# Output of the third column block between the last weight pieces, and another order for the first three attention steps

## The chip, the cores and the metric

The kernel runs on one core of one Trainium2 chip. The metric is the device time of one execution in microseconds (us), as the median of several runs. A profile is one further execution, recorded by the hardware profiler.

## The reference

Windowed attention over a sequence of 768, with the sequence also seen as 24 block summaries of 32 positions each, and behind it a soft mixture of experts. All arithmetic is float32.

```python
k_sum = k.reshape(B, H, nb, 32, D).max(axis=3)           # B,H,S,D = 4,8,768,64; nb = 24
v_sum = v.reshape(B, H, nb, 32, D).mean(axis=3)
scores_l = where(|i-j| < 16, scale * q @ k.T, -1e9)
scores_s = scale * q @ k_sum.T + log(32)
a = softmax(concat([scores_l, scores_s]))                # a / (sum + 1e-9)
x = (a @ concat([v, v_sum])) as [3072, 512]
logits = x @ phi                                         # phi 512 x 32 slots, 8 experts x 4
slot_in = softmax(logits, axis=0).T @ x
slot_out[e] = relu(slot_in[e] @ w1[e]) @ w2[e]           # w1 512 x 1024, w2 1024 x 512
out = softmax(logits, axis=1) @ slot_out                 # 3072 x 512
```

## The kernel before, in words

**The order is written out by hand.** Each engine runs its instructions in the order in which the program issues them (`tc.manual_schedule()`, line 834); semaphores are set from the tiles that are written and read. So a wait of one instruction holds everything behind it on the same engine. All large transfers are issued by SyncE (SP) and share its queue, also in program order; only the constants `cs` come from ScalarE's (line 510).

**Attention: 24 steps.** A step `i` is one third of the queries of four heads (`hb = i // 3`, `tp = i % 3`). Its parts, by the helper that issues them:

- `scores(i)` (line 226): 32 matmuls into two PSUM tiles s0 and s1. Each exists once, so `scores(i+1)` waits until VectorE has read those of step i. A query tile meets its own 64 keys, 32 neighbours and 24 block maxima. The neighbours and the maxima lie in an extra area of `kk` that `k_edge` (line 193) and `k_put` (line 205) fill, for two values of `c` and six query tiles; `scores(i)` reads the query tiles `2*tp` and `2*tp+1`. `k_max` (line 181) finds the maxima on VectorE, in six parts per `hb`.
- `soft_max(i, r)` (line 244) on VectorE for r = 0 and 1, four instructions each, which read s and leave the masked scores and their maximum in SBUF. For r = 0 `soft_exp` (line 259) follows with four ScalarE instructions; for r = 1 GpSimd first subtracts the maximum (`soft_sub`, line 267) and one ScalarE instruction does the rest.
- In the step after: `put_v` (line 347) on GpSimd writes the block sums of v into the tile of values, `trans` (line 271) transposes on TensorE, `evac` (line 278) copies back on ScalarE.
- Two steps after: `values` (line 283) and `norm` (line 301).
- `V0` to `V7`: `v_sum(hb)` (line 320), the block sums of v for one `hb`: 48 matmuls that need the three tiles of values of that `hb`, a copy on ScalarE (line 337), two additions on VectorE into `vsst` (line 340). `PLAN` (line 41) says at which step such pieces begin; the part of an entry in front of the bar is begun and finished in the middle of the step, the part behind the bar is begun at the step's end and finished in the next step, ahead of `soft_max` of r = 1. X, L, T and D are pieces of the routing to experts, later on.

Before the steps stand seven warm-up products (line 506), the first loads (lines 507 to 516), and for `hb` 0 the maxima (line 524), edges (GpSimd, line 525) and `k_put` (VectorE, line 526), then a clearing of `W1ST` on GpSimd (line 527).

**The end.** The first expert layer is 32 weight pieces (line 667), the second is done in three column chunks, a (256 columns, 16 pieces), b and c (128 columns, 8 pieces each). The generator `stage2` (line 695) gives one piece per advance, then three closing advances: a scaling on VectorE (`sos`, line 715), a product on TensorE (`so2`, line 718), a copy on VectorE into `sls` (line 720). `combine` (line 724) makes the output from `sls`, for each block of 128 columns in four advances: the four matmuls of part 0 (256 wide) with two ScalarE copies; two VectorE copies and the output transfer (512 KB); the four matmuls of part 1 (512 wide) with two ScalarE copies; two VectorE copies and two output transfers of 512 KB (four of 256 KB for the very last part). A is two blocks, B and C one each. Six PSUM buffers serve these products. The string `END` (line 68) is the order in which all are advanced: a lower-case letter advances `stage2`, an upper-case one `combine`, the digits of `c1 c2 c3` only mark the closing advances.

Of the kernel before, what the change touches and what calls it, by code (L numbers as in the profile page):

```python
# [16 lines left out]
B, H, S, D = 4, 8, 768, 64  # L17
NT, DM, NS, NE, DF = B * S, H * D, 32, 8, 1024
NB = S // 32
# [3 lines left out]
NTT = 2 * TPS  # L23
# [15 lines left out]


PLAN = {
    0: "| V0",
    2: "| V1",
    5: "| V2",
    6: "X0 X1 |",
# [20 lines left out]

CHUNKS = {"a": (0, 256), "b": (256, 128), "c": (384, 128)}
END = (
    "a a a a a a a a a a a a a a a a a1 b b a2 b b a3 b b A A b A A b A A c A A c b1 c b2 c b3 c "
    "c c c c1 B c2 c3 B B B C C C C"  # L70
)


# [1 line left out]
def attention_soft_moe(  # L75
# [12 lines left out]
    nc = tc.nc  # L88
# [66 lines left out]
    def load_k(hb, pr=None):  # L155
        if hb < HB:
            k = kk[hb % 2][:, K0:EA0]
            c = slice(0, 2 * KP) if pr is None else slice(KP * pr, KP * pr + KP)
            nc.sync.dma_start(out=k[:, c], in_=kx[hb, :, c])

    def load_q(i):
        if i < NSTEP:
            nc.sync.dma_start(out=qb[:, i % NQR], in_=qx[i // TPS, :, i % TPS])

    def load_v(i):
        if i < NSTEP:
            v = vs[i % NV]
            nc.sync.dma_start(out=v.rearrange("p c t h d -> p (c t h d)"), in_=vx[i, :, 0:1040])


    def kview(hb):
        k = kk[hb % 2][:, K0:EA0]
        return k.rearrange("p (r k) -> p r k", r=2)

    def eview(hb, c):
        e0 = (EA0, 0)[c]
        return kk[hb % 2][:, e0 : e0 + NEH].rearrange("p (r t k) -> p r t k", r=2, t=NTT)

    kst = {}

    def k_max(hb, part):
        if hb >= HB:
            return
        if hb not in kst:
            kst[hb] = wk.tile([128, 2, NB], F32, name="ks", bufs=2)
        pr, th = part // 3, part % 3
        nc.vector.reduce_max(  # L187
            out=kst[hb][:, pr, 8 * th : 8 * th + 8],
            in_=kview(hb)[:, pr, 16 + 256 * th : 272 + 256 * th].rearrange("p (b k) -> p b k", k=32),
            axis=AX,  # L190
        )

    def k_edge(hb, eng):
        if hb >= HB:
            return
        k = kview(hb)
        for c in range(2):
            e = eview(hb, c)[:, :, :, 32 * c : 32 * c + 32]
            for half in range(2):
                o = 64 * c + 80 * half  # L200
                src = k[:, :, o : o + 128 * (NTT - 1) + 16]
                src = bass.AP(src.tensor, src.offset, [src.ap[0], src.ap[1], [128, NTT], [1, 16]])
                eng.tensor_copy(out=e[:, :, :, 16 * half : 16 * half + 16], in_=src)  # L203

    def k_put(hb, eng):
        if hb >= HB:
            return
        for c in range(2):
            o = 0 if c else 32
            eng.tensor_copy(  # L210
                out=eview(hb, c)[:, :, :, o : o + NB], in_=kst[hb].unsqueeze(2).broadcast_to([128, 2, NTT, NB])
            )

    def keys(hb, r, c, pr, t):
# [11 lines left out]
    def scores(i):  # L226
        hb, tp = steps[i]
        s = [ps_s.tile([128, 4, 128], F32, name=f"s{r}") for r in range(2)]
        for u in range(4):
            tt, pr = u // 2, u % 2  # L230
            for r in range(2):
                for c in range(2):
                    o = 128 * tt + 64 * c
                    nc.tensor.matmul(  # L234
                        s[r][64 * c : 64 * c + 64, u, :].rearrange("p (a k) -> p a k", a=2),
                        lhsT=qb[64 * r : 64 * r + 64, i % NQR, pr, o : o + 64],
                        rhs=keys(hb, r, c, pr, 2 * tp + tt),
                        start=True,
                        stop=True,
                        tile_position=(64 * r, 64 * c),  # L240
                    )
        ps_[i] = s
# [104 lines left out]
    def put_v(i, c, eng):  # L347
        n0 = 0 if c else 96
        src = vsst[0:NB, i // TPS % 2].rearrange("n h c -> n (h c)").unsqueeze(1)
        eng.tensor_copy(  # L350
            out=vs[i % NV][n0 : n0 + NB, c].rearrange("n t h c -> n t (h c)"), in_=src.broadcast_to([NB, 2, 260])
        )
# [129 lines left out]
    def advance(g):  # L482
        try:
            next(g)
            return True
        except StopIteration:
            return False

    def flush(gs):
        for g in gs:  # L490
            while advance(g):
                pass
# [3 lines left out]
    def begin(names):  # L496
        gs = [pieces_of[n[0]](int(n[1:])) for n in names.split()]
        for g in gs:
            advance(g)
        return gs  # L500
# [7 lines left out]
    load_k(0, 1)  # L508
    load_q(0)
    nc.scalar.dma_start(out=cs, in_=cst)  # L510
    for i in range(TPS):
        load_v(i)
    load_q(1)
    load_q(2)
    load_k(1, 0)
    load_k(1, 1)
# [6 lines left out]
    for part in range(6):  # L523
        k_max(0, part)
    k_edge(0, nc.gpsimd)
    k_put(0, nc.vector)
    nc.gpsimd.memset(W1ST, 0.0)


# [1 line left out]
    for i in range(NSTEP):  # L531
        a, b = i - 1, i - 2
        front, back = (PLAN.get(i, "|")).split("|")
        hb, tp = i // TPS, i % TPS
        now[0] = i
        scores(i)
        if i < TPS:
            for n in ((3, 4), (5,), (6,))[i]:
                load_v(n)
        if i == 0:  # L540
            load_q(3)
        load_q(i + NQR)
        if tp == 2:
            load_k(hb + 2, 0)
        if tp == 0 and hb > 0:
            load_k(hb + 1, 1)
        held = [g for g in held if advance(g)]
        soft_max(i, 0)
        soft_exp(i, 0)
        flush(held)  # L550
        if a >= 0:
            for c in range(2):
                put_v(a, c, nc.gpsimd)
        for n in range(LOADS[i]):
            if now[0] < 19:
                load_piece(True)
        if tp == 2:
            k_put(hb + 1, nc.gpsimd)
        soft_max(i, 1)
        if i < NSTEP - 1:  # L560
            soft_sub(i, 1)
        if tp == 1:
            k_edge(hb + 1, nc.gpsimd)
        if a >= 0:
            trans(a, 0)
            trans(a, 1)
            evac(a, 0)
            evac(a, 1, nc.vector.tensor_copy if i == NSTEP - 1 else None)
        flush(begin(front))
        soft_exp(i, 1)  # L570
        if b >= 0:
            values(b)
            norm(b)
        if tp < 2:
            for part in ((0, 1, 2), (3, 4, 5))[tp]:
                k_max(hb + 1, part)
        held = begin(back)
        if b >= 0:
            load_v(b + NV)
        for _ in range(LOADS[i]):  # L580
            if now[0] >= 19:
                load_piece()
# [80 lines left out]
    for k in range(32):  # L663
        _, e, c = pieces[k]
# [17 lines left out]
    for i in range(2):  # L682
        nc.vector.tensor_copy(
            out=W2ST[i].rearrange("p j (e k) -> p j e k", e=NE)[:, :, :, 0:4],
            in_=ph[:, 128 * i : 128 * i + 128].rearrange("p (j e k) -> p j e k", j=4, e=NE),
# [157 lines left out]
```

## Time and profile before

| | us |
|---|---|
| median of three runs | 193.09 |
| the three runs | 193.09, 191.21, 193.20 |
| the profiled execution's own time | 191.26 |
| its span, first to last instruction | 189.0 |
| mean granted TensorE clock in the span | 0.976 of full |

The span begins with the first instruction and ends with the last; the 2.3 us between it and the execution's own time lie around it. All times below count from the span's start. A step's end is read as the end of its last VectorE instruction that reads scores.

### The profile page before, as it was taken

The numbers are of one execution on the slowest core, as the hardware profiler recorded it, in microseconds if no ns is written. First come the engines' busy times: TensorE is split into PE (matmuls) and PEld (weight loads), VectorE is DVE, ScalarE is ACT, GpSimd is POOL, SyncE is SP. The second block draws the span as 40 slices with busy tenths as digits, with TensorE's granted clock in tenths as the row PEclk, the third lists the DMA queues.
The fourth block names the chain that finished last, engine by engine and source line by source line (L and its number), as shares of the span: only waits on it lengthen the run. The fifth ranks groups of instructions, "written<-read, shape, count | busy, mean of one in ns | idle before, by whom it ended". The sixth has DMA issues, their size and how long they took to land.

```text
span 189.0 us, 7987 instructions
## 1 busy us (share of the span) xinstructions
PE 165.9 (88%) x3201; PEld 130.0 (69%) x3201; DVE 121.1 (64%) x626; ACT 94.4 (50%) x244; POOL 71.9 (38%) x147
## 2 busy tenths in 40 slices
PE   6596999998999979899999898989779989998940
PEld 5394877976968967697798696878357755664720
DVE  1758599686879688848978885864567610135450
ACT  2026667587676677756678577765301000033240
POOL 3425956748544943824854844420020000000000
PEclk9969999999999999999999999999999999999985
DMA  5999989998799998979899999979999999999697
GB/s 193 415 401 400 344 336 299 385 393 312 223 368 386 304 355 262 352 231 297 290 264 389 402 408 408 388 275 394 416 409 404 402 413 408 406 401 396 251 397 269
DMA packets 20628, 66.35 MB, mean 351 GB/s; under 512 B 2288, under 2 KB 2288, under 8 KB 20592
## 3 DMA queue, kind: packets, MB, share of 16 engines
q1 hardware_dynamic: 20448, 65.48, 93.0%
q8 instruction: 25, 0.41, 0.9%
q10 hardware_dynamic: 144, 0.37, 0.5%
q14 instruction: 11, 0.09, 0.1%
HBM read 59.55 MB, written 6.29 MB: 348 GB/s over the span
## 4 chain that ended last, share of the span: by engine, by line
PE 55%; DVE 12%; ACT 12%; issue 4%; POOL 3%; DMA 2%; DVEq 1%; POOLq 0%; ACTq 0%; SPq 0%
PE s L234 8%; PE o L291 8%; PE pt L275 8%; PE hps L667 7%; PE so L705 6%; PE pp L327 5%; DVE p L253 5%; ACT xt L364 4%; PE pp L361 3%; ACT ptr L280 3%; PE op L731 3%; DMA out<-wa 2%; ACT p L263 2%; PE pp L374 2%; PE pp L417 2%
## 5 line engine op out<-in xcount | busy, mean ns | idle before, releaser
L263 ACT ACTIVATE p<-p,m 128x128 f32<-128x128 f32 x100 | 32.0, 391 | 27.3 <-DVE m L253 27.3
L253 DVE CUSTOM_DVE_ANT_0 p<-s,cs 128x128 f32<-128x128 f32 x192 | 42.6, 286 | 4.4 <-PE s L234 4.1
L269 POOL TENSOR_TENSOR p<-m,p 128x512 f32<-128x512 f32 x23 | 23.9, 1038 | 44.0 <-DVE m L253 28.1
L234 PE MATMUL s<-kk,q 64*64 64x128 f32 x768 | 29.9, 280 | 4.2 <-DVE kk L210 2.2
L350 POOL COPY v<-vsst 24x520 f32<-24x520 f32 x48 | 29.4, 612 | 4.4 <-issue 1.6
L234 PEld LDWEIGHTS s<-kk,q 64*64 64x64 f32 x768 | 24.0, 136 | 10.2 <-issue 4.7
L291 PE MATMUL o<-v,ptr 120*64 120x65 f32 (+1 forms) x768 | 27.9, 225 | 1.5 <-DVE x L312 0.9
L291 PEld LDWEIGHTS o<-v,ptr 120*64 120x64 f32 (+1 forms) x768 | 24.6, 138 | 5.6 <-issue 4.6
L275 PE MATMUL pt<-ident,p 128*128 128x128 f32 x192 | 27.9, 282 | 0.6 <-ACT p L265 0.2
L280 ACT COPY ptr<-pt 128x512 f32<-128x512 f32 x47 | 24.7, 571 | 1.7 <-PE pt L275 1.7
L275 PEld LDWEIGHTS pt<-ident,p 128*128 128x128 f32 x192 | 20.4, 140 | 6.2 <-issue 3.3
L187 DVE TENSOR_REDUCE ks<-kk 128x8 f32<-128x256 f32 x48 | 17.0, 410 | 4.3 <-DMA kk<-kx 4.2
L265 ACT ACTIVATE p<-p 128x512 f32<-128x512 f32 x23 | 14.7, 639 | 8.8 <-POOL p L269 8.7
L312 DVE TENSOR_TENSOR x<-o,z 128x256 f32<-128x256 f32 x48 | 18.1, 419 | 0.8
L253 DVE DVE_READ_ACCUMULATOR2_ANT m<- 128x1 f32 x192 | 15.9, 83 | 0.0
L327 PE MATMUL pp<-v,cs 64*64 64x128 f32 x384 | 14.0, 284 | 0.8 <-ACT xt L364 0.7
L327 PEld LDWEIGHTS pp<-v,cs 64*64 64x64 f32 x384 | 12.0, 141 | 1.6 <-ACT xt L364 1.2
L361 PE MATMUL pp<-ident,x 128*128 128x128 f32 x88 | 11.6, 273 | 0.1
L309 DVE TENSOR_SCALAR z<-o 128x8 f32<-128x8 f32 x24 | 4.0, 165 | 11.8 <-PE o L291 11.2
L364 ACT COPY xt<-pp 128x512 f32<-128x512 f32 x21 | 11.4, 595 | 0.0
L203 POOL COPY kk<-kk 128x192 f32<-128x192 f32 x32 | 9.6, 342 | 4.3 <-DMA kk<-kx 4.3
L742 ACT COPY wa<-op 128x256 f32<-128x256 f32 (+1 forms) x3 | 1.2, 445 | 20.0 <-PE op L731 20.0
(134 smaller groups left out, 199.9 us busy)
## 6 DMA issues: line engine op xcount, KB each, us to landing
wa<-w SPq DMA_DIRECT2D x40, 512.0 KB, 7.7
v<-vx SPq DMA_DIRECT2D x24, 520.0 KB, 6.1
kk<-kx SPq DMA_DIRECT2D x16, 400.0 KB, 5.3
q<-qx SPq DMA_DIRECT2D x24, 256.0 KB, 4.8
v<-w SPq DMA_DIRECT2D x7, 512.0 KB, 6.2
kk<-w SPq DMA_DIRECT2D x6, 512.0 KB, 6.9
x<-w SPq DMA_DIRECT2D x5, 512.0 KB, 7.5
out<-v SPq DMA_DIRECT2D x3, 512.0 KB, 4.8
```

The source lines that it names most:

```text
L234: nc.tensor.matmul(s[r][64 * c : 64 * c + 64, u, :].rearrange("p (a k) -> p a k", a=2), lhsT=qb[64 * r : 64 * r + 64, i % NQR, pr, o : o + ...
L253: nc.vector.tensor_tensor_reduce(out=p[:, u, :], in0=s[:, u, :], in1=maskv[:, mk, :], scale=-0.125, scalar=-NEG, op0=ALU.add, op1=ALU.min, ...
L263: nc.scalar.activation(out=p[:, u, :], in_=p[:, u, :], func=AF.Exp, scale=-1.0, bias=m[:, u : u + 1])
L269: nc.gpsimd.tensor_tensor(out=p, in0=m.unsqueeze(2).broadcast_to([128, 4, 128]), in1=p, op=ALU.subtract)
L275: nc.tensor.transpose(pt[:, u, :], p[:, u, :], ident)
L280: (eng or nc.scalar.copy)(out=ptr, in_=ptr_[i, r])
L291: nc.tensor.matmul(o[64 * c : 64 * c + 64, r, u, :], lhsT=ptr[0:K, u, 64 * c : 64 * c + 64], rhs=v[0:K, c, tt, 2 * pr + r, :], start=True, ...
L312: nc.vector.tensor_tensor(out=x[:, r], in0=o[:, r, :, 0:64].rearrange("p (t q) d -> p t q d", t=2), in1=z[:, r].rearrange("p (t q) -> p t ...
L327: nc.tensor.matmul(pv[c][64 * g : 64 * g + 64, 0:128].rearrange("p (h d) -> p h d", h=2), lhsT=cs[64 * c : 64 * c + 64, o : o + 64], rhs=v ...
L350: eng.tensor_copy(out=vs[i % NV][n0 : n0 + NB, c].rearrange("n t h c -> n t (h c)"), in_=src.broadcast_to([NB, 2, 260]))
L361: nc.tensor.transpose(pv[:, 128 * c : 128 * c + 128], x, ident)
L364: (nc.vector.tensor_copy if on_dve else nc.scalar.copy)(out=xt.rearrange("p c t -> p (c t)"), in_=pv)
```

## The change

`END`: of the four advances of B that stood behind `c1`, three are moved up between the last pieces of chunk c, and the fourth stays between `c1` and `c2`. C follows right behind `c3`.

The start: the queries of step 1 are loaded ahead of the three value tiles. `k_put(0)` is split: query tiles 0 and 1 stay on VectorE, tiles 2 to 5 go to GpSimd, ahead of the clearing of `W1ST`. `V0` moves from the end of step 0 into step 1, behind `soft_sub(1, 1)`, and `put_v(0)` follows it there. For `hb` 1 the maxima move from the ends of steps 0 and 1 to the end of step 1 and into step 2, and `k_put(1)` and `k_edge(1)` both stand in step 2 behind `soft_sub(2, 1)`. From step 3 on the order is as before.

```diff
 PLAN = {
-    0: "| V0",
+    1: "V0 |",
...
-    "... b A A c A A c b1 c b2 c b3 c "
-    "c c c c1 B c2 c3 B B B C C C C"
+    "... b A A c A A c b1 c b2 c b3 c B c B c "
+    "B c c1 B c2 c3 C C C C"
...
-    def k_put(hb, eng):
+    def k_put(hb, eng, t0=0, n=NTT):
...
             eng.tensor_copy(
-                out=eview(hb, c)[:, :, :, o : o + NB], in_=kst[hb].unsqueeze(2).broadcast_to([128, 2, NTT, NB])
+                out=eview(hb, c)[:, :, t0 : t0 + n, o : o + NB],
+                in_=kst[hb].unsqueeze(2).broadcast_to([128, 2, n, NB]),
             )
...
+    load_q(1)
     for i in range(TPS):
         load_v(i)
-    load_q(1)
...
-    k_put(0, nc.vector)
+    k_put(0, nc.vector, 0, 2)
+    k_put(0, nc.gpsimd, 2, 4)
     nc.gpsimd.memset(W1ST, 0.0)
...
-        if a >= 0:
+        if a > 0:
             for c in range(2):
                 put_v(a, c, nc.gpsimd)
...
-        if tp == 2:
+        if tp == 2 and hb > 0:
             k_put(hb + 1, nc.gpsimd)
         soft_max(i, 1)
         if i < NSTEP - 1:
             soft_sub(i, 1)
-        if tp == 1:
+        if i == 1:
+            flush(begin(front))
+            front = ""
+            put_v(0, 0, nc.gpsimd)
+            put_v(0, 1, nc.gpsimd)
+        if i == 2:
+            for part in (3, 4, 5):
+                k_max(1, part)
+            k_put(1, nc.gpsimd)
+        if tp == 1 and hb > 0:
             k_edge(hb + 1, nc.gpsimd)
+        if i == 2:
+            k_edge(1, nc.gpsimd)
...
+        if i == 1:
+            for part in (0, 1, 2):
+                k_max(1, part)
-        if tp < 2:
+        if tp < 2 and hb > 0:
             for part in ((0, 1, 2), (3, 4, 5))[tp]:
                 k_max(hb + 1, part)
```

## Rows read from the trace of the kernel before

**Rows 1.** The page's first part: busy us of each engine, with its share.

```profile
PE 165.9 (88%) x3201; PEld 130.0 (69%) x3201; DVE 121.1 (64%) x626; ACT 94.4 (50%) x244; POOL 71.9 (38%) x147
```

**Rows 2.** Stretches of the start (columns: us, busy, granted clock, DMA share, GB/s).

```profile
6.84:9.04 2.20, 0.00 (x0) 0.03 (x1) 2.17 (x5) 0.00 (x0) 1.94 (x5) 1.00 1.02 420
...
9.14:12.54 3.40, 3.40 (x63) 3.35 (x67) 1.28 (x12) 0.93 (x4) 0.00 (x0) 0.50 1.04 399
...
15.00:18.00 3.00, 1.36 (x21) 0.94 (x25) 2.86 (x20) 1.96 (x6) 1.59 (x3) 1.00 1.04 404
```

**Rows 3.** Timeline 7 to 11 us (start us, us, engine, line, operation, count).

```profile
7.43 0.34 POOL L203 COPY kk<-kk 128x192 f32<-128x192 f32 x1
...
7.56 1.38 DVE L210 COPY kk<-ks 128x288 f32<-128x288 f32 x1
...
7.72 1.06 POOL L527 MEMSET W1ST<- 128x1152 f32 x1
...
8.86 0.29 DVE L210 COPY kk<-ks 128x288 f32<-128x288 f32 x1
...
9.04 2.02 PE L234 MATMUL s<-kk,q 64*64 64x128 f32 x29 [2.21 <-DVE kk L210]
```

**Rows 4.** Timeline, DVE and ScalarE of steps 0, 1 and 3.

```profile
12.97 0.08 DVE L253 DVE_READ_ACCUMULATOR2_ANT m<- 128x1 f32 x1
...
14.75 0.24 ACT L337 COPY vp<-pp 88x128 f32<-88x128 f32 x1
...
15.09 0.58 DVE L340 TENSOR_TENSOR vsst<-pp,vp 24x128 f32<-24x128 f32 x2 [0.65 <-ACT vp L337]
...
24.36 0.29 DVE L253 CUSTOM_DVE_ANT_0 p<-s,cs 128x128 f32<-128x128 f32 x1
...
26.05 0.09 DVE L253 DVE_READ_ACCUMULATOR2_ANT m<- 128x1 f32 x1
```

**Rows 5.** Timeline 18 to 28 us: one undisturbed instance of each operation.

```profile
18.61 1.20 POOL L203 COPY kk<-kk 128x192 f32<-128x192 f32 x4
...
21.05 1.54 PE L327 MATMUL pp<-v,cs 64*64 64x128 f32 x48
...
21.11 0.79 POOL L210 COPY kk<-ks 128x288 f32<-128x288 f32 x2
...
21.87 1.03 POOL L269 TENSOR_TENSOR p<-m,p 128x512 f32<-128x512 f32 x1
...
22.41 1.05 PE L234 MATMUL s<-kk,q 64*64 64x128 f32 x32
...
23.40 1.09 PE L275 MATMUL pt<-ident,p 128*128 128x128 f32 x8
...
24.69 1.28 ACT L263 ACTIVATE p<-p,m 128x128 f32<-128x128 f32 x4 [0.98 <-DVE m L253]
...
27.16 1.06 DVE L187 TENSOR_REDUCE ks<-kk 128x8 f32<-128x256 f32 x3
```

**Rows 6.** Timeline of the end, 171 to 183 us.

```profile
171.02 1.14 PE L731 MATMUL op<-lt,sls 32*128 32x512 f32 x8
...
176.63 0.71 PE L731 MATMUL op<-lt,sls 32*128 32x256 f32 x8
...
176.77 0.35 DVE L715 TENSOR_SCALAR sos<-so,rz 128x128 f32<-128x128 f32 x1 [2.06 <-PE so L705]
...
177.80 0.29 DVE L720 COPY sls<-so 128x128 f32<-128x128 f32 x1 [0.68 <-PE so L718]
...
181.44 1.29 DVE L747 COPY v<-op 128x512 f32<-128x512 f32 x2 [0.55 <-PE op L731]
```

**Rows 7.** Stretches of the end (columns as in the second group).

```profile
177.50:179.80 2.30, 2.30 (x16) 1.75 (x17) 1.81 (x5) 1.46 (x4) 0.00 (x0) 1.00 0.25 96
...
179.80:187.60 7.80, 1.94 (x12) 1.06 (x10) 2.38 (x5) 1.84 (x5) 0.00 (x0) 0.72 1.01 394
```

**Rows 8.** The line that issues the output (min/median/max ns, first and last start).

```profile
L751 SPq DMA_DIRECT2D out<-kk x3: 332/333/685, 173.0 to 178.8; - x3
```

More of the change, by code (lines that the diff above doesn't have):

```diff
@@ L68 @@
 END = (
-    "a a a a a a a a a a a a a a a a a1 b b a2 b b a3 b b A A b A A b A A c A A c b1 c b2 c b3 c "
-    "c c c c1 B c2 c3 B B B C C C C"
+    "a a a a a a a a a a a a a a a a a1 b b a2 b b a3 b b A A b A A b A A c A A c b1 c b2 c b3 c B c B c "
+    "B c c1 B c2 c3 C C C C"
 )
```

## The prediction

> **What bounds the kernel now.** I read the page's first part, then the start and the end as timelines, then both as stretches. TensorE is busy for 165.9 of 189.0 us [rows 1]; from step 3 on it hardly pauses, so what makes step 3 earlier should make everything behind it earlier. Two places are left where TensorE or the transfers stand still.
>
> The start. TensorE does nothing from 6.84 to 9.04 us, and the granted clock, 1.00 until then, is 0.50 from 9.14 to 12.54, the lower of its two levels (1.2 GHz) [rows 2]. What ends the pause is the second copy of `k_put(0)` on VectorE. Its first copy takes 1.38 us and the second, of the same shape, 0.29 [rows 3]: the first begins while GpSimd is in its last `k_edge` copy and ends 0.16 us after GpSimd's clearing of `W1ST` (7.72 + 1.06 = 8.78), so it stood behind GpSimd for about 1.09 us. Later VectorE ends step 0 at 13.05 and can begin step 1 only at 15.7, behind V0's additions (15.09 + 0.58), which waited for a ScalarE copy of V0 [rows 4].
>
> The end. From 177.5 to 179.8 the transfers run at a share of 0.25, 96 GB/s; from 179.8 to 187.6 at 394 GB/s, with nothing left for TensorE after the first quarter [rows 7]. The last stretch, 7.8 us, is the output of B and C (2 × 1.57 MB, 8.0 us at that rate): B's first transfer is issued only at 178.8 [rows 8], and the stream picks up about 1.0 us after it.
>
> **Part 1: the first scores.** VectorE's share of `k_put(0)` falls to a third, two copies of 96 elements. Undisturbed, a copy of 288 takes 0.29, so the two cost at most 0.3 together at one third to one half of that each. Whether they are undisturbed is the question, since GpSimd now goes from its last `k_edge` copy to two copies of its own, 192 elements, 0.34 each and 0.29 apart as `k_edge` shows, and then to the clearing. If VectorE gets in behind the `k_edge` copy, at 7.77, it is done at 8.1, or at 8.4 if one GpSimd copy comes between its two; scores begin 0.6 to 0.9 us earlier than 9.04. If it again stands behind all that GpSimd has queued, that ends at 7.72 + 2 × 0.29 + 1.06 = 9.36, VectorE ends near 9.6, and scores are 0.5 us late. So the bounds are −0.9 and +0.5. I take −0.7: before, GpSimd's next instruction waited for nothing and only wrote; now it waits for the maxima as VectorE does, and reads.
>
> The Trainium skill (SBUF — State Buffer, section "Who interferes with whom") says that GpSimd and a VectorE copy of this kind share one pair of ports under an exclusive lock, and that issue order decides who blocks. The first copy agrees with the lock: 1.38 us against 0.29. It does not quite agree with the order, as VectorE asked at 7.56 and the clearing began at 7.72, yet the clearing went first; By the order of asking VectorE's two copies would end at 8.1 and the term be −0.9; by the order of the row, at 9.6 and +0.5, which is the second rival below.
>
> Query tiles 2 to 5, now GpSimd's, are ready by 8.4 to 8.7 and not read before step 1. `load_q(1)` is moved past three value loads on SP: the values land later by 262 KB, 0.6 us at about 410 GB/s, and V0, their first reader, now comes about one step later. Both cost nothing.
>
> **Part 2: steps 0 to 3.** I count from E0, the end of step 0's maxima on VectorE (13.05 before), with the durations of [rows 5].
>
> Before: step 3 ends at 26.14 [rows 4], E0 + 13.1.
>
> Changed. Step 1's scores start at E0 and take 1.1; VectorE has nothing else queued and runs step 1's eight instructions from E0+1.1 to 2.9 (1.78, as step 3 took from 24.36 to 26.14 [rows 4]). TensorE does V0 under it (1.54, to E0+2.7) and the transposes (1.09, to 3.8). ScalarE must finish step 1's four exponentials (1.28, to 3.1), then V0's copy (0.24); VectorE adds from 3.45 to 4.05, then three parts of maxima (1.06) to 5.1. Scores of step 2 are ready at 4.9; VectorE runs step 2 from 5.1 to 6.9. GpSimd does `put_v(0)` and `put_v(1)` between 4.1 and 6.7, then `soft_sub(2, 1)` (1.03) from 7.0 to 8.05, `k_put(1)` (0.79) to 8.85, whose maxima VectorE has ready at 8.0, and `k_edge(1)` (1.20) to 10.05. Scores of step 3, which need these edges, run from 10.2 to 11.25, and step 3's maxima from 11.25 to 13.0. So step 3 ends at E0 + 13.0, as before: the gap behind step 0 is closed (step 1 starts 1.1 behind E0, not 2.6), but the edges for `hb` 1, which GpSimd made early, are now at the end of its queue, and TensorE, through with V1 at E0+8.65, waits 1.5 us for them. The reorder by itself brings 0 (bounds −0.6, if GpSimd's queue runs with no gaps, and +0.7, if one `put_v` or the values of V1, loaded in a saturated stretch, come late). What it does is carry E0 on; and the scores of step 0 set E0.
>
> **The clock.** Before, step 0's scores ran at the lower level: 2.02 us for 29 matmuls [rows 3] against 1.05 for 32. With the pause cut to 1.4 us they may run at full speed, −0.9. But V0 no longer follows them: TensorE pauses again for the 1.8 us of step 0's maxima. The stretch from 15 to 18, busy for 1.36 of 3.0 us, kept its 1.00 [rows 2], the one from 6.84 did not. The new stretch of two pauses lies between; I take it that one of the two score blocks runs at the lower level, as one did before: 0, with −0.9 and +0.9 as bounds.
>
> **Part 3: the end.** Before, chunk c's last matmul ended by 176.77, where VectorE scales it [rows 6]. B's matmuls, 0.71 and 1.14, now come ahead of it, so the scaling is at 176.77 + 1.85 = 178.6 and ends at 178.95. Then VectorE has B's fourth advance queued, two copies of 512, 1.29 as the last pair took, and only then the copy into `sls`, 0.29: 180.55. The product `so2` hides under the copies; TensorE has nothing left to fill this with and stands still for some 1.5 us. C's first matmuls end at 181.3, its first output leaves near 182.0, and its last copies (1.29, behind a pair half as wide) end near 183.4.
>
> What it buys is in the transfers. B's first 512 KB is issued near 176.8 and goes into the gap, right behind A. B's other two are issued at 179.7 and 180.3, about where they were, as VectorE's copies wait behind the scaling. The stream therefore picks up at about 180.6 and has 2.62 MB left, 6.65 us at 394 GB/s: 187.2, against 187.6. I take −0.4. Bounds: −1.3, if B's first transfer is saved in full; +0.9, if C's own copies, one microsecond later, set the end.
>
> **Sum.** −0.7 (first scores) + 0 (reorder) + 0 (clock) − 0.4 (end) = −1.1. Against the profiled execution's own 191.26 (span 189.0 and 2.3 around it) that is 190.2. The executions shown stand at two levels, 191.2 and 193.1 to 193.2, two of four at each, with the median of the three runs, 193.09, on the upper. I start from their mean, 192.2: **191.1 us**.
>
> **The rivals.**
>
> *Full speed in both score blocks.* The forecast with −0.9 for the clock: −2.0, 190.2 us. For it: the longest pause of TensorE becomes 1.8 instead of 2.2. Against it: two pauses follow closely. Chance 0.18.
>
> *VectorE stays behind GpSimd's queue.* It decides once VectorE's copies end after 9.15, where they ended before; nothing in [rows 3] excludes it, since there VectorE lost the one boundary between two GpSimd instructions that it met. Scores +0.5; TensorE then has paused for 2.7 us, runs step 0's scores at the lower level, pauses again and runs step 1's there too, which before were at 1.00 (+0.9); the end −0.4. Sum +1.0: 193.2 us, slower than before. Chance 0.25.
>
> *The start gains nothing.* Step 3 waits for GpSimd's edges longer than the 1.5 us above, by the 0.7 that step 0 won (the values of V1 or `put_v` late by as much). What speaks for it: every link of that chain stands on one engine's queue. Only the end is left: −0.4, 191.8 us. Chance 0.15.
>
> The forecast itself has 0.42; its own range, by the bounds of its terms, is 189.8 to 192.2.
>
> **How the numbers follow.** The range takes in the rivals and the two levels of the runs: 189.0 to 193.6. A difference of about 1% is what a measurement of this kernel tells from none. Faster by over 1% (1.9 us) needs the first rival or the lucky part of the forecast: 0.12 + 0.12, and 0.06 for a change of level between runs, 0.30. Slower by over 1% is the upper half of the second rival: 0.13. Within 1%: 0.57.
>
> **What would show it.** Right: the two VectorE copies of `k_put(0)` end before 8.5 and the first score matmul follows; step 1's maxima start 1.1 to 1.2 behind the end of step 0's; step 3's scores wait for GpSimd's last edge copy; at the end the slack stretch around 178 has a transfer in it and VectorE copies B between the scaling and the copy into `sls`. Wrong: a `k_put(0)` copy of over 1 us, a clock of 0.50 while step 1's scores or V0 run, or C's last copies and not the stream of transfers setting the end.

## The result, and the profile after

| | before | changed |
|---|---|---|
| median us | 192.97 (20 runs, 190.84 to 194.96) | 191.22 (20 runs, 189.98 to 192.65) |
| profiled execution's own time, us | 191.26 | 190.07 |
| its span, us | 189.0 | 188.2 |
| mean granted clock in the span | 0.976 | 0.986 |

The ratio is 0.9916 (95% interval 0.9894 to 0.9939): faster by 0.84%. Ratios here and below are of executions in the fast state alone, so a ratio can differ from the quotient of the two medians, which are of all executions. The forecast was 191.1 us, with within 1% of before as the likeliest outcome. The time came out as said; the gain is larger than the 1.1 us of the sum, and the base it was taken from was too low (below).

The timeline of the start, the changed kernel, against [rows 3] and [rows 4]:

```profile
7.41 0.34 POOL L203 COPY kk<-kk 128x192 f32<-128x192 f32 x1
7.53 0.28 DVE L210 COPY kk<-ks 128x96 f32<-128x96 f32 x1
7.70 0.34 POOL L210 COPY kk<-ks 128x192 f32<-128x192 f32 x1
7.73 0.38 DVE L210 COPY kk<-ks 128x96 f32<-128x96 f32 x1
...
7.91 1.43 PE L235 MATMUL s<-kk,q 64*64 64x128 f32 x32 [1.21 <-DVE kk L210]
...
8.28 1.06 POOL L529 MEMSET W1ST<- 128x1152 f32 x1
...
11.04 0.08 DVE L254 DVE_READ_ACCUMULATOR2_ANT m<- 128x1 f32 x1
...
12.21 0.29 DVE L254 CUSTOM_DVE_ANT_0 p<-s,cs 128x128 f32<-128x128 f32 x1 [1.09 <-PE s L235]
...
19.72 1.21 POOL L203 COPY kk<-kk 128x192 f32<-128x192 f32 x4
...
20.58 0.67 PE L328 MATMUL pp<-v,cs 64*64 64x128 f32 x16 [1.72 <-DMA v<-vx]
...
21.06 1.11 PE L235 MATMUL s<-kk,q 64*64 64x128 f32 x32
...
22.28 0.29 DVE L254 CUSTOM_DVE_ANT_0 p<-s,cs 128x128 f32<-128x128 f32 x1
...
23.97 0.08 DVE L254 DVE_READ_ACCUMULATOR2_ANT m<- 128x1 f32 x1
```

VectorE's two copies take 0.28 and 0.38 us, between GpSimd's, and the clearing of `W1ST` is behind all of them. The first scores begin at 7.91 (9.04 before, −1.13) and step 0's maxima end at 11.12 (13.05, −1.93: the matmuls themselves run at full speed). Step 1's maxima begin 1.09 us behind that. Step 3's scores begin at 21.06, right behind the last third of V1's matmuls (20.58), which had waited 1.72 us for its values; GpSimd's last edge copy had ended shortly before, at 19.72 + 1.21 = 20.93. Step 3 ends at 24.05 (26.14, −2.09).

The chain that ended last, followed back from step 3's scores, goes through the landing of those values (start us, us):

```profile
11.69 8.84 DMA v<-vx
...
21.24 0.94 PE s L235 x32
```

The third value tile of `hb` 1 is issued at 11.69 and lands at 20.5. Neither the end of step 0 nor GpSimd's edges are on that chain.

The same stretches as [rows 2] (busy us of PE, PEld, DVE, ACT, POOL with counts, granted clock, DMA share, GB/s), and one later in the span:

```profile
6.84:9.04 2.20, 1.13 (x30) 1.01 (x32) 1.23 (x5) 0.00 (x0) 2.20 (x7) 1.00 1.03 422
9.14:12.54 3.40, 1.92 (x57) 1.53 (x55) 2.11 (x19) 1.54 (x5) 1.24 (x2) 1.00 1.03 397
15.00:18.00 3.00, 3.00 (x76) 2.59 (x72) 2.97 (x20) 2.51 (x7) 2.57 (x6) 1.00 1.03 400
...
138.00:142.00 4.00, 3.46 (x34) 2.05 (x37) 2.53 (x6) 0.63 (x1) 1.06 (x1) 0.57 1.03 407
```

The start keeps the full clock throughout; from 138 to 142 us it is 0.57 in the mean, where the kernel before had 1.00 (next fence, its stretch of the same bounds). The first expert layer begins there. Its first matmuls, before:

```profile
138.00:142.00 4.00, 3.07 (x37) 2.40 (x37) 2.62 (x8) 0.00 (x0) 1.06 (x1) 1.00 1.03 410
...
140.90 9.27 PE L667 MATMUL hps<-wa,W1ST 128*32 128x256 f32 x168 [0.54 <-DVE rz L471]
```

and, from the changed kernel's timeline:

```profile
139.12 10.66 PE L684 MATMUL hps<-wa,W1ST 128*32 128x256 f32 x168 [0.54 <-DVE rz L472]
```

Of the 2.09 us won by step 3 the layer's start still has 1.78 (140.90 to 139.12); between these two executions its first 168 matmuls give 1.39 back to the clock (9.27 to 10.66). That is not a price of the change. In the run below that has the kernel before and only a later clearing, the same matmuls take as long:

```profile
141.17 10.66 PE L668 MATMUL hps<-wa,W1ST 128*32 128x256 f32 x168 [0.54 <-DVE rz L471]
```

The profiled execution of the kernel before was a lucky one there: only 2 of the 61 executions of it that ran beside the experiments had a mean clock of 0.975 or more, against its 0.976.

The end, the changed kernel's timeline against [rows 6]:

```profile
173.04 0.34 DVE L732 TENSOR_SCALAR sos<-so,rz 128x128 f32<-128x128 f32 x1
...
178.37 0.35 DVE L732 TENSOR_SCALAR sos<-so,rz 128x128 f32<-128x128 f32 x1 [1.91 <-PE so L722]
178.64 0.68 DVE L764 COPY v<-op 128x512 f32<-128x512 f32 x1
179.24 0.68 DVE L764 COPY x<-op 128x512 f32<-128x512 f32 x1
179.38 0.33 SPq L768 DMA_DIRECT2D out<-v  x1
179.83 0.28 DVE L737 COPY sls<-so 128x128 f32<-128x128 f32 x1
180.17 2.37 PE L748 MATMUL op<-lt,sls 32*128 32x256 f32 x16 [0.84 <-DVE sls L737]
```

and its stretches, against [rows 7]:

```profile
177.50:179.80 2.30, 1.26 (x22) 0.67 (x18) 1.43 (x3) 1.07 (x2) 0.00 (x0) 1.00 0.58 232
179.80:187.60 7.80, 2.37 (x16) 1.08 (x16) 2.46 (x6) 1.82 (x4) 0.00 (x0) 0.92 0.86 336
```

As a measure of the end alone I take the time from the scaling of chunk b (173.04 here, 173.43 before) to the last instruction: 15.20 us against 15.56. That leaves out everything that the start did. From 180.30 on, 0.9 us behind the issue of B's second transfer, the stream runs to its end without a gap:

```profile
180.30:186.70 6.40, 2.24 (x16) 0.95 (x16) 2.14 (x4) 1.82 (x4) 0.00 (x0) 0.97 1.01 393
```

### The profile page after: what moved, and what is told of

Read it like the earlier page. It is cut to its first block, busy times and chain, and to the rows that moved or that the text cites. A ratio compares the mean times of both kernels' runs of the same rounds, so it can differ in the third digit from the quotient of the medians.

```text
span 188.2 us, 7987 instructions
## 1 busy us (share of the span) xinstructions
PE 164.9 (88%) x3201; PEld 125.3 (67%) x3201; DVE 120.2 (64%) x626; ACT 94.7 (50%) x244; POOL 72.8 (39%) x149
## 4 chain that ended last, share of the span: by engine, by line
PE 40%; DMA 22%; ACT 13%; DVE 12%; issue 4%; POOL 4%; SPq 2%; POOLq 0%; ACTq 0%; DVEq 0%
DMA wa<-w 11%; DMA v<-vx 9%; PE s L235 7%; PE o L292 6%; PE pt L276 6%; PE hps L684 4%; ACT xt L365 4%; PE pp L328 4%; ACT ptr L281 4%; ACT p L264 3%; DVE p L254 3%; DMA out<-wa 2%; PE pp L375 2%; PE op L748 2%; PE pp L418 2%
## 5 line engine op out<-in xcount | busy, mean ns | idle before, releaser
L235 PE MATMUL s<-kk,q 64*64 64x128 f32 x768 | 28.5, 274 | 3.0 <-DVE m L254 1.5
L235 PEld LDWEIGHTS s<-kk,q 64*64 64x64 f32 x768 | 22.6, 133 | 9.2 <-issue 4.9
L328 PE MATMUL pp<-v,cs 64*64 64x128 f32 x384 | 13.3, 273 | 2.5 <-DMA v<-vx 1.7
L328 PEld LDWEIGHTS pp<-v,cs 64*64 64x64 f32 x384 | 11.0, 133 | 3.5 <-DMA v<-vx 2.0
L365 ACT COPY xt<-pp 128x512 f32<-128x512 f32 x21 | 11.4, 593 | 0.0
L684 PE MATMUL hps<-wa,W1ST 128*32 128x256 f32 x168 | 10.7, 419 | 0.5 <-DVE rz L472 0.5
```

The source lines that it names most:

```text
L235: nc.tensor.matmul(s[r][64 * c : 64 * c + 64, u, :].rearrange("p (a k) -> p a k", a=2), lhsT=qb[64 * r : 64 * r + 64, i % NQR, pr, o : o + ...
L328: nc.tensor.matmul(pv[c][64 * g : 64 * g + 64, 0:128].rearrange("p (h d) -> p h d", h=2), lhsT=cs[64 * c : 64 * c + 64, o : o + 64], rhs=v ...
L365: (nc.vector.tensor_copy if on_dve else nc.scalar.copy)(out=xt.rearrange("p c t -> p (c t)"), in_=pv)
L684: nc.tensor.matmul(hps[32 * j : 32 * j + 32, :], lhsT=W1ST[:, c, 32 * e : 32 * e + 32], rhs=t[:, j, :], start=(k == 0), stop=(k == 31), ti ...
```

## The experiments

Ratios are to runs of the kernel before on the same chip.

### Each half alone

**The new `END` in the kernel before.**

```diff
-    "... c b3 c c c c c1 B c2 c3 B B B C C C C"
+    "... c b3 c B c B c B c c1 B c2 c3 C C C C"
```

> The kernel before with the new order of the end alone. My theory: the end gives 0.4 us, a ratio of 0.998 to the kernel before; the three parts of B's output that come early put one transfer of 512 KB into the slack stretch around 178 us, and the last stretch of transfers ends 0.3 to 0.5 us earlier relative to the scaling of chunk c. Rival 1, the end is most of the change's gain: 0.993. Rival 2, C's later copies eat it: 1.000 or above.

Measured: 193.39 us (10 runs) against 193.49, ratio 0.9995 (0.9955 to 1.0034). In its trace, 15.17 us from the scaling of chunk b to the end: the end does what was forecast, and it is too small for ten runs to tell from nothing. The interval leaves out rival 1's 0.993.

**The new start with the old `END`.**

```diff
-    "... c b3 c B c B c B c c1 B c2 c3 C C C C"
+    "... c b3 c c c c c1 B c2 c3 B B B C C C C"
```

> The changed kernel with the old order of the end: all edits of the start and nothing else. My theory: the rest of the change's gain, a ratio of 0.993 to 0.995 to the kernel before; first scores at 7.9 us, step 3's maxima from 22.3 as in the changed kernel. Rival, the end is most of the gain: 0.998 or above.

Measured: 192.09, ratio 0.9964 (0.9919 to 1.0008), 15.52 us at the end. Its first scores begin at 8.04 at full speed, but the granted clock is low from 10.5 to 13.9 us, so step 1's scores take 2.49 us. Step 3's maxima begin at 23.26, not 22.28: GpSimd's last edge copy ends at 22.09 (20.93 in the changed kernel), and V1's values too come later (its last third begins at 21.28, not 20.58). The instructions of the start are those of the changed kernel; the clock is not. The interval just reaches 1, so the start's gain by itself is likely but not shown.

### The two parts of the start

**The changed kernel with all of `k_put(0)` on VectorE again.**

```diff
-    k_put(0, nc.vector, 0, 2)
-    k_put(0, nc.gpsimd, 2, 4)
+    k_put(0, nc.vector)
     nc.gpsimd.memset(W1ST, 0.0)
```

> The changed kernel with all of k_put(0) on VectorE again, so that GpSimd goes from its last edge copy straight to the clearing of W1ST. My theory, the first scores carry the start and the reorder gives nothing: the first VectorE copy takes 1.3 to 1.4 us again, scores start near 9.0, and step 3's maxima end 13.0 behind the end of step 0's, at 26.0; ratio to the kernel before 0.998 (the end alone). Rival, the reorder of V0 and the maxima is the gain: ratio 0.993 to 0.995, step 3's maxima end by 25 with scores still at 9.0.

Measured: 193.94, ratio 1.0017 (0.9976 to 1.0058). The two copies take 1.60 us together, the scores begin at 9.41, step 3's maxima at 25.64, so that they end near 27.4 and not at the expected 26.0, and the clock is low from 10.3 to 17.1. The new order without the split wins nothing, not even with the new `END`.

**The kernel before with the split alone.**

```diff
-    k_put(0, nc.vector)
+    k_put(0, nc.vector, 0, 2)
+    k_put(0, nc.gpsimd, 2, 4)
     nc.gpsimd.memset(W1ST, 0.0)
```

> The kernel before with the split of k_put(0) alone. My theory: VectorE's two copies end by 8.2 and scores start at 7.9; step 1's maxima still wait for V0's additions, step 3's end 13.1 behind the end of step 0's, so about 1.1 to 1.9 us earlier than before; ratio 0.992 to 0.995. Rival, V0's additions hold step 1 at its old place (step 1 at 15.7 whatever step 0 does): ratio 1.000 and the gain needs the reorder.

Measured: 193.45, ratio 1.0011 (0.9964 to 1.0059). The scores begin early (8.26, at full speed), and then this, in its timeline:

```profile
11.44 0.67 PE L328 MATMUL pp<-v,cs 64*64 64x128 f32 x16 [0.68 <-DMA v<-vx]
...
13.74 1.07 DVE L187 TENSOR_REDUCE ks<-kk 128x8 f32<-128x256 f32 x3 [2.28 <-DMA kk<-kx]
...
15.33 0.29 DVE L254 CUSTOM_DVE_ANT_0 p<-s,cs 128x128 f32<-128x128 f32 x1
```

VectorE is through with step 0 at 11.47, and next in its queue stand the maxima for `hb` 1, whose keys land only at 13.7: it waits 2.28 us for them. Step 1 begins at 15.33 instead of 15.70, and step 0's gain is gone: step 3 begins at 23.99 and so ends 14.3 us behind E0. The expectation, a ratio of 0.992 to 0.995, failed; its rival came out, though V0's additions are not what holds step 1 longest. In the kernel before the same wait for the keys is 0.32 us, small enough to overlook:

```profile
13.37 1.07 DVE L187 TENSOR_REDUCE ks<-kk 128x8 f32<-128x256 f32 x3 [0.32 <-DMA kk<-kx]
```

**The split and, with it, the maxima, `k_put(1)` and `k_edge(1)` of `hb` 1 moved as in the change; `V0` and the queries of step 1 at their old places, old `END`.**

```diff
-        if tp == 2:
+        if tp == 2 and hb > 0:
             k_put(hb + 1, nc.gpsimd)
...
+        if i == 2:
+            for part in (3, 4, 5):
+                k_max(1, part)
+            k_put(1, nc.gpsimd)
-        if tp == 1:
+        if tp == 1 and hb > 0:
             k_edge(hb + 1, nc.gpsimd)
+        if i == 2:
+            k_edge(1, nc.gpsimd)
...
+        if i == 1:
+            for part in (0, 1, 2):
+                k_max(1, part)
-        if tp < 2:
+        if tp < 2 and hb > 0:
```

> The kernel before with the split, and with the maxima, k_put and k_edge for hb 1 moved as in the change, but V0 in its old place and the queries of step 1 behind the values. My theory after the first runs: the wall of the old order is the landing of the keys for hb 1 at 13.4 us, on which VectorE's maxima wait ahead of step 1; with these behind step 1, step 1 starts at 13.5 to 14.0 (V0's values land at 11.4, its additions end near 13.6) and step 3 near 23; ratio 0.994 to 0.997. Rival, V0 in front of step 1 is the wall: step 1 stays at 15.0 or later, ratio 1.000.

Measured: 191.63 (4 runs), ratio 0.9899 (0.9828 to 0.9969): not told apart from the whole change. In its timeline the wait for the keys is gone and V0's is left:

```profile
13.52 0.58 DVE L341 TENSOR_TENSOR vsst<-pp,vp 24x128 f32<-24x128 f32 x2 [2.04 <-ACT vp L338]
...
14.13 0.29 DVE L254 CUSTOM_DVE_ANT_0 p<-s,cs 128x128 f32<-128x128 f32 x1
```

Step 1 begins at 14.13 and step 3 at 23.16, where the changed kernel has 12.21 and 22.28. So of what the new order does, moving the maxima for `hb` 1 from VectorE's queue ahead of step 1 to behind it is the part that lets the early scores through. What V0's move adds is not shown: step 3 begins 0.88 us later than in the changed kernel, but V1's last third, which waits for its values in both, begins 0.82 later too (21.40 against 20.58), and the ratios don't tell the two apart.

### What VectorE stood behind

**The kernel before with the clearing moved behind step 0's `soft_sub`.**

```diff
     k_put(0, nc.vector)
-    nc.gpsimd.memset(W1ST, 0.0)
...
+        if i == 0:
+            nc.gpsimd.memset(W1ST, 0.0)
```

> The kernel before with the clearing of W1ST moved behind soft_sub(0, 1) on GpSimd, nothing else. If the first copy's 1.38 us was the wait behind the clearing, VectorE's two copies of 288 elements take about 0.3 each behind GpSimd's last edge copy and end near 8.3 us, with nothing split, and scores start about 0.9 us earlier, near 8.1. Rival, the first copy is slow by itself (its first use, or the maxima that it waits for): it stays above 1 us. Step 1's maxima start between 15.0 and 15.4 in any case, as in the run with the split alone, since the maxima for hb 1 wait for their keys until 13.4.

Measured: one run, 192.5 us against a median of 193.54. Both copies are short:

```profile
7.87 0.37 DVE L210 COPY kk<-ks 128x288 f32<-128x288 f32 x1
...
8.17 0.29 DVE L210 COPY kk<-ks 128x288 f32<-128x288 f32 x1
```

and the scores begin at 8.34. Then the wait for the keys follows again, 2.24 us, and step 1's maxima begin at 15.3.

**The changed kernel with the clearing ahead of GpSimd's two copies.**

```diff
     k_put(0, nc.vector, 0, 2)
-    k_put(0, nc.gpsimd, 2, 4)
     nc.gpsimd.memset(W1ST, 0.0)
+    k_put(0, nc.gpsimd, 2, 4)
```

> The changed kernel with the clearing of W1ST between the last edge copy and GpSimd's own part of k_put(0). If an instruction of GpSimd that waits for nothing and only writes goes ahead of VectorE, VectorE's first copy takes 1.1 to 1.3 us, scores start near 9.0 and the ratio to the kernel before is about 0.998 to 1.000, as without the split. If VectorE got in because its copies are smaller, or by chance of order, both end by 8.2 and the ratio is that of the change, 0.992.

Measured: 194.5 (10 runs) against 193.54, ratio 1.0045 (0.9999 to 1.0092). Its timeline:

```profile
7.89 0.34 POOL L203 COPY kk<-kk 128x192 f32<-128x192 f32 x1
...
8.03 1.28 DVE L210 COPY kk<-ks 128x96 f32<-128x96 f32 x1
...
8.18 1.06 POOL L528 MEMSET W1ST<- 128x1152 f32 x1
```

A copy of 96 elements takes 1.28 us, though it asked 0.15 us ahead of the clearing; the scores begin at 9.40 and the clock is low from 11.4 to 18.2. So VectorE loses to the clearing with the split too, when the clearing comes next on GpSimd. The scores begin 1.37 us behind the moment at which VectorE asked, against 1.48 in the kernel before (7.56 to 9.04): in this trace they are not later for it. Step 0's scores run at full speed (1.22 us), and the low clock falls on step 1's (2.49). The copy's 1.28 us is as expected; the ratio lies above the expected 0.998 to 1.000, but its interval reaches that.

**The kernel before with two GpSimd copies that wait for nothing, ahead of the clearing** (they write into `W1ST`, which the clearing then overwrites):

```diff
+    for _ in range(2):
+        nc.gpsimd.tensor_copy(out=W1ST[:, 0, 0:192], in_=kk[0][:, K0 + 64 : K0 + 256])
     nc.gpsimd.memset(W1ST, 0.0)
```

> The kernel before with two extra copies of 128x192 on GpSimd, SBUF to SBUF, which wait for nothing, between the last edge copy and the clearing of W1ST. If VectorE gets in ahead of an instruction of GpSimd that reads SBUF and loses only to the clearing, its first copy ends within 0.45 us and the second goes ahead of the clearing too, both by 8.8. If what let it in was that GpSimd's part of k_put waited for the maxima, VectorE loses again and its first copy takes 1.8 to 2.0 us.

Measured: one run, 192.6 against a median of 192.79. Its timeline:

```profile
7.93 0.37 DVE L210 COPY kk<-ks 128x288 f32<-128x288 f32 x1
...
8.09 0.41 POOL L528 COPY W1ST<-kk 128x192 f32<-128x192 f32 x1
...
8.97 1.06 POOL L529 MEMSET W1ST<- 128x1152 f32 x1
```

VectorE gets in, and its second copy ends at 8.67, ahead of the clearing. GpSimd's next instruction here waits for nothing, as the clearing did, and is a copy. So it isn't the waiting that let VectorE in, but that the neighbour is a copy and not the clearing. Which property of the clearing does it (that it reads nothing, its length of 1.06 us against 0.34, or the kind of instruction) no run tells.

### The end once more

**The changed kernel with all four advances of B one piece of chunk c earlier,** so that the last of them, too, stands ahead of `c1`.

```diff
-    "... c b3 c B c B c B c c1 B c2 c3 C C C C"
+    "... c b3 B c B c B c B c c1 c2 c3 C C C C"
```

> The changed kernel with all four advances of B one piece of chunk c earlier, so that VectorE's last two copies of B end before chunk c is scaled. If these copies between the scaling and the copy into sls are what makes C late, C's first matmuls start 0.8 to 0.9 us earlier behind the scaling, and from the scaling of chunk b to the last instruction it is 14.5 to 14.8 us instead of 15.2; ratio to the kernel before 0.989. If the transfers alone set the end, 15.2 stays within 0.2.

Measured: 190.84 (4 runs), ratio 0.9881 (0.9805 to 0.9956), 14.68 us from the scaling of chunk b to the end, 0.52 less than the change has. Its timeline:

```profile
178.06 0.69 DVE L764 COPY v<-op 128x512 f32<-128x512 f32 x1 [1.33 <-PE op L748]
...
178.82 0.33 SPq L768 DMA_DIRECT2D out<-v  x1
...
179.27 0.34 DVE L732 TENSOR_SCALAR sos<-so,rz 128x128 f32<-128x128 f32 x1
...
180.25 0.29 DVE L737 COPY sls<-so 128x128 f32<-128x128 f32 x1 [0.64 <-PE so L735]
```

The two executions can be compared only from a point that both share; I take the scaling of chunk b (173.76 in this one, 173.04 in the change). Counted from it, B's last two transfers are issued 1.28 us earlier (the first at 5.06, against 6.34) and the copy into `sls`, with no copies of B ahead of it, starts 0.30 earlier (6.49 against 6.79); C's first output is issued 0.29 earlier (8.43 against 8.72). Behind the scaling of chunk c, C's matmuls start 0.47 earlier (1.33 against 1.80), about half of what was expected. The stream of transfers now has a gap, until C's first output, issued at 182.19, fills it:

```profile
182.20:183.00 0.80, 0.77 (x4) 0.00 (x0) 0.69 (x1) 0.66 (x2) 0.00 (x0) 1.00 0.25 97
183.00:187.10 4.10, 0.00 (x0) 0.00 (x0) 0.69 (x1) 0.50 (x1) 0.00 (x0) 1.00 0.99 384
```

In the change there is no such gap: its end is set by the stream. Here B's transfers are 1.28 us ahead, the stream then waits for C, and 0.52 of the 1.28 reaches the end. So neither of the two expectations holds as it was put: the time is that of the first, and both the transfers and C's copies have a part in it. The same `END` gives 14.98 in the last run below, so the gain at the end is 0.2 to 0.5 us; in the ratio it does not stand out.

### The clock ahead of the expert layer

**The changed kernel once more,** beside the next two on one chip.

> The changed kernel once more, as the reference for the two runs that follow it on the same chip: ratio 0.988 to 0.994 to the kernel before, with the runs at two levels again, near 190.3 us without a stretch of the lower clock behind the attention part and near 191.5 with one.

Measured: 190.98 us (12 runs) against 192.79, ratio 0.992 (0.9884 to 0.9957). A mean clock of 0.986 to 0.988 came in 5 of the 12 (189.99 to 191.19 us) and 0.963 to 0.979 in the other 7 (190.37 to 192.15), so the two levels overlap this time. That the faster level goes without the low clock behind the attention part was wrong: the profiled execution, 190.38 us at 0.986, has it (its stretches are shown with the next run).

**Seven products of `ident` with itself, into a PSUM tile that nobody reads, at the waits of the routing ahead of the expert layer** (added work, no part of the result):

```diff
+    def warm(n):
+        for _ in range(n):
+            nc.tensor.matmul(wt_ps[:, 0, :], lhsT=ident, rhs=ident, start=True, stop=True)
...
     flush(begin("T4"))
+    warm(1)
...
     advance(R)
+    warm(3)
     flush(gt)
...
     advance(R)
+    warm(1)
     advance(R)
...
-    flush([slots()])
+    gs = slots()
+    advance(gs)
+    warm(2)
+    flush([gs])
```

> The changed kernel with seven extra 128x128 products on TensorE, whose result nobody reads, in the places between 132 and 139 us where it waits for VectorE and ScalarE. If the low clock near 138 to 142 us follows these waits, it is gone from most runs: the granted clock of the whole span rises to 0.985 or above in most, and the median falls by 0.5 to 0.9 us against the changed kernel. If the low clock does not depend on them, the share of runs with a mean clock under 0.98 stays near one half, and the time stays or grows by up to 0.3 us.

Measured: 189.02 (6 runs), ratio 0.9816 (0.9759 to 0.9872), 1.96 us below the changed kernel on that chip. The stretches of the changed kernel, second profile:

```profile
132.00:139.20 7.20, 5.24 (x59) 2.79 (x47) 3.69 (x14) 1.10 (x5) 0.29 (x1) 0.99 1.03 415
139.20:142.00 2.80, 2.76 (x28) 1.61 (x32) 2.10 (x4) 0.52 (x1) 0.78 (x1) 0.50 1.02 402
```

and of this one, with the layer's first matmuls from its timeline:

```profile
132.00:139.40 7.40, 7.21 (x81) 4.69 (x73) 3.62 (x14) 1.11 (x5) 0.22 (x1) 1.00 1.03 414
139.40:142.00 2.60, 2.59 (x49) 1.88 (x52) 2.17 (x4) 0.25 (x1) 0.85 (x1) 1.00 1.03 405
...
139.51 9.27 PE L696 MATMUL hps<-wa,W1ST 128*32 128x256 f32 x168
```

The layer begins about 0.3 us later than in that second profile (139.24) and its first 168 matmuls take 9.27 us, where they took 10.85. By the profiles that is 1.3 us; the medians differ by 1.96, more than twice the 0.5 to 0.9 expected, and no trace shows the rest. Four of the six executions have a mean clock of 0.985 or above, as expected. This version beats both kernels. The waits alone do not bring the low clock each time: without the products TensorE is busy for 5.2 of the 7.2 us ahead of the layer in every profile, and three of twelve (the kernel before, the clearing put first, the maxima moved with `V0` in place) keep the full level behind them. With the products both profiles keep it.

**Both, the products and B earlier.**

> The changed kernel with both the extra products and B one piece of chunk c earlier. If the two add up: 1.0 to 1.4 us below the changed kernel, ratio to the kernel before 0.985 or below. If the extra products do nothing: 0.5 us below it, 0.989.

Measured: 189.57 (6 runs), ratio 0.9836 (0.9777 to 0.9894), 14.98 us at the end. It is 1.41 below the changed kernel, but no better than the products alone; the intervals overlap. Whether moving B is worth anything beside them stays open.

## Why the prediction was right, and where it wasn't

**First scores, −0.7: right in kind, too small.** Measured −1.13, outside the bound of −0.9. The step that failed is the size of the best case. "What ends the pause is the second copy" holds for all but the first two of the 32 matmuls. These two begin 0.10 us behind the first copy: before at 9.04, behind 7.56 + 1.38 = 8.94; after at 7.91, behind 7.81; with the late clearing at 8.34, behind 8.24. Up to 9.29 before and up to 8.24 after, they are alone (the first line is of the kernel before, the second of the changed one):

```profile
9.04 0.57 PE L234 MATMUL s<-kk,q 64*64 64x128 f32 x2 [2.21 <-DVE kk L210]
...
7.91 0.40 PE L235 MATMUL s<-kk,q 64*64 64x128 f32 x2 [1.21 <-DVE kk L210]
```

The third begins about 0.15 us behind the second copy, at 9.30 before and 8.25 after, −1.05. The second copy ends at 8.11 instead of 9.15, which is the best case that I gave, 8.1; but I counted its gain from 9.04, where the first matmul begins, and not from 9.15, and then took −0.7 and not the best case.

The reason given was half right. "Now it waits ... and reads" held two causes; the free-running copies and the clearing put first tell them apart: waiting is not needed, and a clearing next in GpSimd's queue goes ahead of a VectorE copy that asked first.

The Trainium skill (SBUF — State Buffer, "Who interferes with whom") gives the exclusive lock, and every row above agrees: 1.28 and 1.38 us against 0.28. Its rule that issue order decides agrees where GpSimd has copies, and not where it has the clearing, which began 0.15 us after VectorE's copy and ran first. The measurements decide.

**Reorder, 0: the number right, the wait and the claim about the order before wrong.** Step 3 ends at E0 + 12.93 (forecast 13.0) and step 1 begins at E0 + 1.09 (1.1). But step 3's scores do not wait for the edges, which end at 20.93 (forecast E0 + 10.05, 21.17): they come right behind V1, whose last third waited 1.72 us for its values and began at 20.58. The forecast had V1 through at E0 + 8.65, 19.77, and kept the late values as a bound only. Edges and values were late almost together, so the agreement of 12.93 with 13.0 is in part luck, and by this trace a still earlier E0 would gain nothing unless the values, too, came earlier. It is no single case: in five other runs with the new start V1's last third waits for its values too, 1.08 to 1.96 us; in two of them (the old `END`, the seven products) the edges end later still, at 22.09 and 21.17, while the scores have begun at 21.77 and 20.93.

What failed besides is the account of the order before. I named V0's additions as what holds step 1; the larger hold is that the keys of `hb` 1 land at 13.4 to 13.8 us and the maxima that need them stand on VectorE's queue ahead of step 1. The 13.1 us behind E0 were read as a length of work; in part they were a landing time, as the expectation for the split alone found out. That the earlier scores need the reorder was right: without it they reached nothing. The split alone gives 1.0011, the new order with the new `END` but without the split 1.0017, and all three together 0.9916: the parts don't add.

**The clock, 0: the sum near it by two errors.** I expected one of the two score blocks at the lower level. In the profiled execution both ran at full speed, as in the first rival: the 0.80 us between −1.13 and −1.93. The 1.39 us that went back at the first expert layer, a place that I had not looked at, belong to the two executions and not to the change (above). Over many runs the clock is worth more than 0: the kernel before had a mean granted clock of 0.959 to 0.977 in all of 61 executions, the changed one 0.986 to 0.988 in 9 of 20 (189.98 to 190.86 us) and 0.963 to 0.979 in the other 11 (191.22 to 192.65).

**The end, −0.4: right.** −0.36 by 15.56 to 15.20 us, and the four runs of the halves and the start's parts agree: 15.52 and 15.53 with the old `END` (new start, split alone), 15.17 twice with the new one. As forecast, B's last copies lie between the scaling and `sls` and TensorE waits there; counted from the scaling of chunk b, that of chunk c was at 5.33 (forecast 5.2) and `sls` ended at 7.07 (7.1). The stream of transfers and not C's copies sets the end.

**The sum.** In the profiled executions −1.19 us (191.26 to 190.07) against −1.1, which is luck: it is −1.78 at the layer's start, +1.39 from the layer's clock, −0.36 at the end and −0.44 outside the span (2.27 us around it before, 1.83 after). By the medians it is −1.75, by the ratio's interval −1.2 to −2.0. My base of 192.2, from four executions, was 0.8 below the median of twenty; a base too low and a gain too small met at 191.1, by luck as well. Without the layer's clock the traces give −1.78 − 0.36 = −2.1; why the medians give less is not shown. The forecast's own range, 189.8 to 192.2, is not the sum of its terms' bounds, −3.7 to +3.0; how it was narrowed is not said there.

**The rivals.** VectorE behind GpSimd's clearing was real, but the rival as put, VectorE behind all that GpSimd has queued, was not met, since GpSimd's copies came ahead of the clearing. With the clearing put first the ratio of 1.0045 is about +0.9 us (none to +1.8) against the +1.0 forecast; the size is near by other terms, as step 0's scores ran at full speed there and the low clock lay behind them. "The start gains nothing" came true for the split alone, by the landing keys and not by GpSimd's edges. The late values of V1, which it has in brackets, set step 3 in the changed kernel, but without taking the gain.

**Open.** The run with the new start and the old `END` had a low clock at 10.5 us that the five other profiles with the start as changed did not have, with the same instructions up to there; its ten executions all have a mean clock of 0.968 to 0.976. It ran on another chip than the repeat of the change, so whether the chip, the execution or the program did it is not settled.

## What to carry to other kernels

Before a gain is carried from one step to the next, look in each queue for the small wait on a transfer behind it: 0.32 us of waiting before was a wall of 2.28 once the work ahead of it was faster, and with that one out of the way the next transfer, V1's values, held TensorE for 1.72. On a path that sets the start, keep GpSimd's large clearings behind VectorE's short copies. Compare two executions from a point that both share, not by the time since their start. And look for the clock at the entry of every stage bound by TensorE, not only where the change is, and in more than one execution: seven small products that nobody reads were worth 1.96 us by the medians, about as much as the whole change.

## What the runs showed of the hardware

- VectorE's copies and GpSimd's copies into the same memory take turns, one instruction each: a VectorE copy that meets one in flight ends 0.06 to 0.16 us behind it (in the changed kernel GpSimd's last edge copy ends at 7.75 and VectorE's first copy at 7.81, GpSimd's next at 8.04 and VectorE's second at 8.11; with the late clearing 8.08 and 8.24). At the boundary to GpSimd's clearing VectorE lost every time that it met it: 1.38 us before, 1.28 with the clearing put first, and 1.60 for two copies without the split.
- In the second profile of the change the clock fell at 139.2 us, behind a stretch in which TensorE had been busy for 5.24 of 7.20 us; it kept its full level through the same work when the gaps were filled (7.21 of 7.40). The share alone does not decide it: in the profile of the kernel before it held behind 5.19 of the 7.20 us up to 140.90, and at the start of the changed kernel it held through 9.14 to 12.54, busy for 1.92 of 3.40 us.
- The same instructions do not always get the same clock: the changed kernel's twenty executions spread over 2.7 us, and their mean clock over 0.963 to 0.988.
